# Two attention layers and two long convolutions: the second attention front in a fixed order, powers and reciprocals on ScalarE, the last norms row by row

## The chip, the cores and the metric

The kernel runs on one core of one Trainium2 chip. A core has a matrix engine (TensorE, PE in the profile, its weight loads PEld), three engines for elementwise work (VectorE or DVE, ScalarE or ACT, GpSimd or POOL) and SyncE (SP), whose queue issues nearly all DMA transfers here. Each engine takes its instructions in the order of its own queue and waits on semaphores for the others. The metric is the device time of one launch in microseconds (us), the median of several runs.

## The reference, cut to what matters

```python
def _A_ref(x, wqkv, wo):                      # S=2048, D=512, 32 heads of 16
    q, k, v = split(x @ wqkv)
    idx = pos[:, None] - 2 * arange(8)        # 8 keys, every second position back
    logits = einsum("bhsd,bhswd->bhsw", q, k[idx]) * 16 ** -0.5   # masked before 0
    attn = softmax(logits)
    return (einsum("bhsw,bhswd->bhsd", attn, v[idx])) @ wo

def _B_ref(u, A, B, C, log_dt, Dskip):        # L=2048, D=512, N=128
    K = einsum("dn,dnl,dn->dl", C, exp(dt * A * l), dt * B).real  # a kernel of length L
    return irfft(rfft(pad(u)) * rfft(pad(K)))[:L] + u * Dskip     # causal convolution

x = x + _A_ref(layernorm(x)); x = x + _B_ref(layernorm(x))
x = x + _A_ref(layernorm(x)); x = x + _B_ref(layernorm(x))
```

Both layers of a kind share their weights, so the convolution kernel and its spectrum are made once.

## The kernel before, in words

The residual x stays in SBUF as `x_sb`, 16 rows a = 0 to 15 of 128 positions by 512 features. Position is split as 16 p + a, so a shift by 2w positions is a shift by 2w rows of a tile, with 14 extra rows in front that hold the same data one partition further (`kT_ext`, `v_ext`).

**Attention, class `LayerA`.** The front works on blocks of four rows: statistics (`row_stats`), `ln_begin` (mean, variance, the power -0.5 by GpSimd, L103), `ln_end` (the shift `ln_nb`, L110), `ln_apply`, PE transposes (`front_t`), key projection with its evacuation to `kT` (`front_k`), and the shifted copy of the keys (`front_ext`). `core` then runs in two halves. The first takes quarters q of four rows and quarters ft of the features: DVE forms all products of queries and the 8 shifted keys (`mult`, tile `prod`), PE sums them per head into the logits L (`lsum`), and between them the projections of queries and values are dealt out by a fixed share (`proj`). For each quarter the maximum (`mx`), the exponential (`sub_exp`) and the normalisation (`norm_p`, with a DVE reciprocal, L334) follow. The second half loops over rows n = 0 to 15: DVE product `pv_mult(n)` (tile `pav`, two buffers), then on PE `pv_sum(n)` (tile `po`) and `out_proj(n-1)`, which adds the residual on PE. ScalarE takes the result back to `x_sb` with its sum and sum of squares; for rows 14 and 15 DVE takes the statistics (`bn_stats`, L77) and ScalarE copies. The next norm is woven in: `u_begin`, `u_end` and `u_apply` act on groups of rows 0-3, 4-7, 8-11, 12-13 and 14-15 and write `u`, the input of the convolution. In the first layer, a dictionary of events adds other work at named places of the loop: sine tables (`gx`, `gw`, `gs`), the load and reordering of the convolution kernel (`k_half_load`, `K`).

**Convolution, class `FftB`.** A Fourier transform as matrix products in two stages. `forward` walks steps s: `f1` (first stage, 16 matmuls into a PSUM tile of four buffers), evacuation by ScalarE or DVE (`evac`, by a running cost), `f2` 11 steps later, and for the data `u_f2` with two DVE products by the kernel's spectrum (`u_mult`, tiles t). In the first layer the kernel itself (`ka`) goes through the transform first, and each part of its spectrum is also written to DRAM. `kf_load` brings spectra to a ring of buffers, `ahead` of their use. `i1` and `i2` are the inverse stages; `i2` adds into `x_sb`. `middle` holds the inverse for the first half of the features.

**What sets the order.** Within `manual_schedule` the instructions of DVE, ScalarE, PE and SP run in the order in which the program emits them. That holds for all parts but one: the second attention front, between the first convolution and the second `core` (L1215 to L1229), is ordered by the framework. There each block of four rows is taken whole as its rows come out of `i2` (`rows_done`).

Of the kernel before, what the change touches and what calls it, by code (L numbers as in the profile page):

```python
# [19 lines left out]
P = 128  # L20
S = 2048
D = 512
# [5 lines left out]
EPS = 1e-5  # L28
MAN = {ET.DVE, ET.Activation, ET.PE, ET.SP}
# [12 lines left out]
EV = dict(act=0.93, dve=1.16)  # L42
# [32 lines left out]
def row_stats(nc, lnst, x_row, a, eng):  # L75
    if eng == "dve":
        nc.vector.bn_stats(lnst["bn"][:, a, :], x_row)  # L77
    else:
        nc.scalar.activation(lnst["junk"][:], x_row, ACT.Identity, accum_out=lnst["s1"][:, a:a + 1])
        row_sumsq(nc, lnst, x_row, a)  # L80
# [6 lines left out]
def ln_begin(nc, pool, lnst, a0, a1, eng):  # L87
    n = a1 - a0
    rstd = pool.tile([P, n], F32, name="ln_rstd")
    if eng == "dve":  # L90
        ag = pool.tile([P, n, 2], F32, name="ln_ag")
        for a in range(n):
            nc.vector.bn_aggr(ag[:, a, :], lnst["bn"][:, a0 + a, :])
        var, mean, ms = ag[:, :, 1], ag[:, :, 0], -1.0
    else:
# [5 lines left out]
        var = veps[:]  # L101
    nc.vector.tensor_scalar(rstd[:], var, EPS, None, ALU.add)  # L102
# [22 lines left out]
class LayerA:  # L125


    def __init__(self, tc, nc, consts, lnst, A_wqkv, A_wo, layer, xnT, nq):
# [10 lines left out]
        self.ps_l = self.wv = None  # L139

# [11 lines left out]
    def front_q(self, q):  # L152
        for ft in range(NDT):
            self.qproj1(q, ft, self.qT[q], self.ps_pj, "pp")

    def front_open(self):
# [5 lines left out]
        self.ps_pj = self.fctx.enter_context(tc.tile_pool(name=f"a{l}_ps_pj", bufs=2, space=PSUM, side="right"))  # L162
        self.nc.gpsimd.memset(self.kT[:, :, 0:14, 0:1], 0.0)
# [8 lines left out]
    def front_block(self, b, x_rows, st_eng, ln_eng, ev_eng, ext):  # L172
        nc, lnst = self.nc, self.lnst
        if st_eng == "dve":
            for a in range(4):
                row_stats(nc, lnst, x_rows[:, a, :], b * 4 + a, st_eng)
        self.front_apply(b, x_rows, ln_block(nc, self.fp, lnst, b * 4, b * 4 + 4, st_eng), ln_eng)
        self.front_t(b, ev_eng[0:2])
        self.front_k(b, ev_eng[2:])
        if ext is not None:  # L180
            for ft in range(NDT):
                self.front_ext(b, ext, ft)

    def front_apply(self, b, x_rows, rn, ln_eng, out=None):
        self.xn = self.fp.tile([P, 4, D], BF16, name="xn") if out is None else out
# [3 lines left out]
    def front_t(self, b, ev_eng):  # L189
        nc, xn = self.nc, self.xn  # L190
# [8 lines left out]
    def front_k(self, b, ev_eng, fts=range(NDT)):  # L199
        nc = self.nc  # L200
        for ft in fts:
            pp = self.ps_pj.tile([P, 512], F32, name="pp", tag="pp")
# [57 lines left out]
    def core(self, x_sb, u, ev=None, nprod=0):  # L260
# [14 lines left out]
        with ExitStack() as c2:  # L275
# [10 lines left out]
            ps_o = c2.enter_context(tc.tile_pool(name=f"a{l}_ps_o", bufs=2, space=PSUM))  # L286

# [36 lines left out]
            def norm_p(q):  # L324
# [6 lines left out]
                nc.vector.tensor_tensor(ssum[:], s2[:, :, 0:1, :], s2[:, :, 1:2, :], ALU.add)  # L331
                rs = wk.tile([P, 4, 1, H], BF16, name="rs")
                with nc.allow_low_precision("softmax normaliser in bf16 (attention weights are bf16)"):
                    nc.vector.reciprocal(rs[:], ssum[:])  # L334
# [25 lines left out]
            def out_proj(a):  # L360
# [6 lines left out]
                if a >= 14:  # L367
# [6 lines left out]
            def u_begin(a0, a1, eng):  # L374
                lns[a0] = (ln_begin(nc, wk, lnst, a0, a1, eng), a1)

            def u_end(a0):
                lns[a0] = (ln_end(nc, wk, lns[a0][0]), lns[a0][1])

            def u_apply(a0, rows):  # L380
                rstd, nb = lns[a0][0]
                for a in rows:
                    ln_apply(nc, u[:, :, a, :], x_sb[:, a, :].rearrange("p (q r) -> p q r", r=4), rstd, nb, a - a0,
                             "dve" if a % 2 else "act")
# [20 lines left out]
            for q, ft in slots:  # L405
                if q == 1 and ft == 0 and 1 not in self.qT:
                    while 1 not in self.qT or projs[0][0] is q_proj:
                        proj(1)
                mult(q, ft)
# [6 lines left out]
                if ft == 0 and q > 0:  # L416
                    proj(0.5)
                    acc -= 0.5
                    sub_exp(q - 1)
                if ft == 3 and q > 0:  # L420
                    norm_p(q - 1)
            proj(100)
            linit(3)
            for n in range(16):
# [3 lines left out]
                if n in (2, 10):  # L428
# [3 lines left out]
                if n in (6, 10):  # L432
                    u_begin(n - 6, n - 2, "act")
                if n in (7, 11):
                    u_end(n - 7)
                if n in (8, 9, 12, 13):
                    b0 = 0 if n < 10 else 4
                    r0 = b0 + (0 if n in (8, 12) else 2)
                    u_apply(b0, range(r0, r0 + 2))
                if n == 14:  # L440
                    u_begin(8, 12, "act")
# [11 lines left out]
            u_end(8)  # L453
            u_begin(12, 14, "act")
            out_proj(15)
            u_apply(8, range(8, 12))
            u_end(12)
            u_apply(12, range(12, 14))
            u_begin(14, 16, "dve")
            u_end(14)  # L460
            u_apply(14, range(14, 16))
# [143 lines left out]
class FftB:  # L605
# [72 lines left out]
    def kf_load(self, n):  # L678
# [10 lines left out]
        if self.kf_ring is None:  # L689
            self.kf_ring = [pool.tile([P, 4, 2, DQG, EC], BF16, name=f"kf_ring{i}")  # L690
                            for i, pool in enumerate((self.ring_pool, self.ring2))]
        kc = self.kf_ring[n // 4 % 2][:, n % 4]
# [64 lines left out]
    def forward(self, srcs):  # L757
# [3 lines left out]
        lag = NQT + 3  # L761
        self.kf = {}
        n_u = 0
        for s in range(len(F2) + lag):
            if s == lag + len(F2) - NG * NEC:
                for n in range(self.ahead):
                    self.kf_load(n)
            self.u_mult()
            if s < len(F1):
                self.f1(*F1[s])  # L770
            if s >= lag:
                key, g, ec = F2[s - lag]
                if key == "ka":
# [10 lines left out]
    def middle(self, done=None):  # L784
        self.i1(1, 0)
        self.i1(1, 1)
        for t in range(NA // 4):
# [4 lines left out]
            if done is not None:  # L792
                done(t)
# [321 lines left out]
def kernel(  # L1115
# [23 lines left out]
    with tc.tile_pool(name="ctmp", bufs=1) as tmp:  # L1139
        consts = build_a_consts(tc, nc, cpool, tmp)  # L1140
    lnst = dict(s1=cpool.tile([P, NA], F32, name="ln_s1"), s2=cpool.tile([P, NA], F32, name="ln_s2"),
                bn=cpool.tile([P, NA, 6], F32, name="ln_bn"), junk=cpool.tile([P, D], BF16, name="ln_junk"),
# [149 lines left out]
```

## Time and profile before

| | |
|---|---|
| median of 3 runs | 495.63 us (495.64, 492.5, 495.63) |
| profiled execution, its own time | 492.67 us |
| its span | 490.8 us |
| PE busy | 363.8 us (74%), granted clock 0.947 |
| DVE busy | 417.1 us (85%) |
| ACT busy | 332.6 us (68%) |
| POOL busy | 35.0 us (7%) |
| first kernel generation and first front | 0 to 128 us |
| first attention, its halves | 128 to 159, 159 to 228 |
| first convolution with the kernel's spectrum | 228 to 299 |
| second front | 299 to 332 |
| second attention, its halves | 332 to 369, 369 to 433 |
| second convolution | 433 to 491 |

The span is the time from the first to the last instruction; the launch adds 1.9 us to it here. Busy shares are means over stages with different limits, so the prediction reads each stage by itself. A line such as L354 is a line of the kernel printed above; "out<-in" names the tiles that an instruction writes and reads; the bracket behind a timeline row gives how long its engine was idle before it and what ended that.

### The profile page before, as it was taken

What the parts mean: (1) busy time and instruction counts of PE and PEld (TensorE: products, weight loads), DVE (VectorE), ACT (ScalarE), POOL (GpSimd) and SP (SyncE); (2) the same over time, 40 slices, a digit from 0 to 9 for tenths busy, and PEclk for the clock granted to TensorE, in tenths of its full rate; (3) what the DMA queues carried; (4) which work ended last, traced back from release to release, by engine and by line L of the source; (5) the groups of instructions that cost most, each with busy time, mean ns of one, the idle gap of its engine ahead of it and who ended that gap; (6) DMA issues with size and microseconds to landing.
All of it is one profiled execution on the core that took longest, in us unless ns stands there. A gap on an engine that the chain in (4) does not pass through costs nothing.

```text
span 490.8 us, 12670 instructions
## 1 busy us (share of the span) xinstructions
PE 363.8 (74%) x5434; PEld 273.6 (56%) x5470; DVE 417.1 (85%) x583; ACT 332.6 (68%) x535; POOL 35.0 (7%) x38
## 2 busy tenths in 40 slices
PE   1000237888999787796996894889997998958796
PEld 1000116564855666575985793444555686747795
DVE  7799979999999998985896968838999999748974
ACT  5999688856365667957897970674552557759873
POOL 2000102000000002121000000100000022210000
PEclk9999987999999899989899999799997899979899
DMA  8901610112015735522265523531022044022715
GB/s 219 369 1 21 65 43 1 45 19 54 9 22 158 243 96 186 229 61 87 94 236 182 188 84 98 162 116 56 3 77 74 2 174 172 1 87 77 233 61 152
DMA packets 57403, 52.22 MB, mean 106 GB/s; under 512 B 28829, under 2 KB 45826, under 8 KB 56066
## 3 DMA queue, kind: packets, MB, share of 16 engines
q1 hardware_dynamic: 57202, 51.27, 33.8%
q8 instruction: 43, 0.70, 0.6%
q10 hardware_dynamic: 144, 0.13, 0.2%
q14 instruction: 14, 0.11, 0.1%
HBM read 30.28 MB, written 13.24 MB: 89 GB/s over the span
## 4 chain that ended last, share of the span: by engine, by line
PE 44%; DVE 22%; ACT 18%; DMA 5%; issue 4%; SPq 3%; POOL 2%; DVEq 0%; ACTq 0%; POOLq 0%
PE pp L204 6%; PE po L354 6%; DVE pav L346 6%; PE pq L145 5%; PE pb L653 4%; PE pq L299 4%; DVE t L706 4%; PE pk L1039 3%; PE L L257 3%; PE pb L660 2%; DVE prod L250 2%; POOL ln_rstd L103 2%; PE pq L366 2%; ACT ws L957 2%; PE pb L732 2%
## 5 line engine op out<-in xcount | busy, mean ns | idle before, releaser
L354 PE MATMUL po<-ident,pav 128*128 128x128 bf16 x1024 | 67.1, 227 | 15.4 <-DVE pav L346 15.4
L354 PEld LDWEIGHTS <-pav 128*128 128x128 bf16 x1024 | 62.7, 102 | 23.6 <-DVE pav L346 20.2
L346 DVE TENSOR_TENSOR pav<-attn,v_ext 128x4096 bf16<-128x4096 bf16 x32 | 72.9, 2283 | 0.2 <-PE po L354 0.2
L250 DVE TENSOR_TENSOR prod<-qT,kT_ext 128x4096 bf16<-128x4096 bf16 x29 | 65.8, 2286 | 3.2 <-PE L L257 3.1
L103 POOL TENSOR_TENSOR ln_rstd<-ln_rstd,ln_mh 128x4 f32<-128x4 f32 (+1 forms) x18 | 29.4, 1632 | 280.4 <-DVE ln_rstd L102 234.5
L357 ACT CAST oT<-po 128x512 bf16<-128x512 f32 x32 | 18.5, 577 | 29.6 <-PE po L354 29.6
L204 PE MATMUL pp<-xnT,kT_ext 128*128 128x512 bf16 x124 | 32.6, 405 | 7.4 <-ACT xnT L197 5.9
L660 PE MATMUL pb<-a1s,w_sb 128*128 128x64 bf16 x768 | 31.3, 198 | 7.3 <-DVE a1s L642 4.4
L716 ACT CAST ub<-pb 128x1024 bf16<-128x1024 f32 x32 | 32.5, 1053 | 6.1 <-DVE t L706 5.9
L195 PE MATMUL pt<-ident,x_blk 128*128 128x128 bf16 x64 | 5.6, 241 | 41.5 <-ACT x_blk L120 41.5
L1039 PE MATMUL pk<-B_t,A_t 128*64 128x84 bf16 (+1 forms) x512 | 25.1, 209 | 12.5 <-issue 9.3
L731 PE MATMUL pb<-Wp,t 128*128 128x128 bf16 x256 | 31.9, 222 | 3.2 <-DVE t L706 2.3
L660 PEld LDWEIGHTS <-w_sb 128*128 128x128 bf16 x768 | 27.2, 101 | 10.5 <-DVE a1s L642 4.7
L301 ACT CAST v_ext<-pq 128x512 bf16<-128x512 f32 x32 | 18.7, 585 | 20.4 <-PE pq L299 20.4
L732 PE MATMUL pb<-WpJ,t 128*128 128x128 bf16 x256 | 31.6, 223 | 1.2 <-DVE t L706 1.1
L257 PEld LDWEIGHTS <-prod 128*128 128x128 bf16 x928 | 27.4, 96 | 8.9 <-DVE prod L250 2.7
L1039 PEld LDWEIGHTS <-A_t 128*64 128x64 bf16 (+1 forms) x512 | 22.9, 109 | 15.8 <-issue 12.6
L366 PE MATMUL pq<-wop,oT 128*128 128x512 bf16 x112 | 30.4, 386 | 1.0 <-issue 0.2
L145 PE MATMUL pq<-xnT,kT_ext 128*128 128x512 bf16 x120 | 29.6, 381 | 0.6 <-issue 0.3
L642 DVE CAST a1s<-pb 128x1024 bf16<-128x1024 f32 x21 | 25.0, 1222 | 5.8 <-PE pb L653 5.7
L299 PE MATMUL pq<-wv,xnT 128*128 128x512 bf16 x120 | 29.6, 379 | 0.4
L642 ACT CAST a1s<-pb 128x1024 bf16<-128x1024 f32 x27 | 26.8, 1024 | 4.2 <-PE pb L653 3.5
(211 smaller groups left out, 862.6 us busy)
## 6 DMA issues: line engine op xcount, KB each, us to landing
w_sb<-w_dram SPq DMA_DIRECT2D x8, 1024.0 KB
w_dram<-w_zero SPq DMA_DIRECT2D x1, 4096.0 KB
kf_ring<-kf_dram SPq DMA_DIRECT2D x16, 256.0 KB
kf_ring<-kf_dram SPq DMA_DIRECT2D x32, 128.0 KB
v_ext<-v_ext SPq DMA_DIRECT2D x4, 784.0 KB
x_blk<-in_A_x_dram SPq DMA_DIRECT2D x4, 512.0 KB
kT_ext<-in_A_wqkv_dram SPq DMA_DIRECT2D x4, 512.0 KB
x_sb<-in_A_x_dram SPq DMA_DIRECT2D x4, 512.0 KB
```

The lines of the kernel that those rows point to most:

```text
L145: nc.tensor.matmul(pq[:], lhsT=self.wqk[:, dt, ft * P:(ft + 1) * P], rhs=self.xnT[:, dt, q * 512:(q + 1) * 512], start=(dt == 0), stop=(dt ...
L204: nc.tensor.matmul(pp[:], lhsT=self.wqk[:, dt, D + ft * P: D + (ft + 1) * P], rhs=self.xnT[:, dt, b * 512:(b + 1) * 512], start=(dt == 0), ...
L250: nc.vector.tensor_tensor(pr, self.qT[q][:, ft].unsqueeze(1).to_broadcast([P, W, 4, P]), kap, ALU.mult)
L257: self.nc.tensor.matmul(L[:, al, w, ft * 8:(ft + 1) * 8], lhsT=pr[:, w, al, :], rhs=self.c["ind8"][:], start=False, stop=True, skip_group_ ...
L299: nc.tensor.matmul(pp[:], lhsT=xnT[:, dt, a * P:(a + 1) * P], rhs=wv[:, dt, :], start=(dt == 0), stop=(dt == NDT - 1))
L346: nc.vector.tensor_tensor(pv[:], attn[:, n % 4].unsqueeze(2).to_broadcast([P, W, DH, H]), vap, ALU.mult)
L354: nc.tensor.matmul(po[:, ft, :], lhsT=pvf[:, w, ft * P:(ft + 1) * P], rhs=ident[:], start=(w == 0 and ft == 0), stop=(w == W - 1), skip_gr ...
L366: nc.tensor.matmul(pw[:], lhsT=oT[:, ftp, :], rhs=wo[:, ftp, :], start=False, stop=(ftp == NDT - 1))
L642: (nc.scalar.copy if eng == "act" else nc.vector.tensor_copy)(dst, src)
L660: nc.tensor.matmul(p2[:, j, :], lhsT=self.w2[:, ec * EC + j, :], rhs=a1s[:, ec * EC + j, :], start=True, stop=True)
L732: nc.tensor.matmul(p3[:, j, :], lhsT=t2[:, dql, :], rhs=wpj_r, start=False, stop=True)
L1039: nc.tensor.matmul(o, lhsT=lhs, rhs=Bt[:, ri, c * CH + ql].rearrange("p b g -> p (b g)"), start=(not half and j % 4 == 0 and ri == 0), sto ...
```

## The change

- **Powers on ScalarE.** `ln_begin` can take the power as Ln (with the epsilon as bias) and Exp (scale -0.5) on ScalarE; in the loops all groups but rows 0-3 do, and the whole second front. The softmax reciprocal becomes Ln and Exp (scale -1). It moves with the three adds ahead of it into `recip`, one or two products earlier than the rest of `norm_p`. The table set that holds both functions is loaded by an instruction written out at two places.
- **Last norms.** Groups become 0-3, 4-7, 8-10, 11-12 and then single rows 13, 14, 15. `u_begin` and `u_end` stand together where ScalarE has the power. Row 13's statistics are taken by DVE too. In the first layer the single rows are handed to `forward` and run behind its steps 1 to 3.
- **Second front.** Written out by hand: statistics in halves (`half_stats`), the first half inside `middle`; two of the four `i2` of the second half add on PE and evacuate on ScalarE; blocks are interleaved; one of two transposed tiles per block is evacuated by DVE; the last block's keys and the first queries go into the first four slots of `core`.
- **Spectra.** `kf_load` starts four steps earlier in the first layer with `ahead` 4; the ring of the second layer has 7 slots instead of 8. Some events of the first loop are one place earlier, the first sine behind the kernel load.

```diff
-EV = dict(act=0.93, dve=1.16)
+EV = dict(act=0.93, dve=1.2)
...
+def half_stats(nc, lnst, x_sb, t, g):
+    for a in range(4 * t, 4 * t + 4):
+        nc.vector.bn_stats(lnst["bn"][:, a, g, :], x_sb[:, a, g * (D // 2):(g + 1) * (D // 2)])
...
+    if rs == "act":
+        nc.scalar.activation(rstd[:], var, ACT.Ln, bias=EPS)
+        nc.scalar.activation(rstd[:], rstd[:], ACT.Exp, scale=-0.5)
+        return rstd, mean, ms
...
-            def norm_p(q):
+            def recip(q):
...
+                ls = wk.tile([P, 4, H], F32, name="ls")
+                nc.scalar.activation(ls[:], ssum[:, :, 0, :], ACT.Ln)
                 rs = wk.tile([P, 4, 1, H], BF16, name="rs")
-                with nc.allow_low_precision("softmax normaliser in bf16 (attention weights are bf16)"):
-                    nc.vector.reciprocal(rs[:], ssum[:])
+                nc.scalar.activation(rs[:, :, 0, :], ls[:], ACT.Exp, scale=-1.0)
+                st[q]["rs"] = rs
+
+            def norm_p(q):
+                ex, rs = st[q]["ex"], st[q]["rs"]
                 attn = wk.tile([P, 4, W, H], BF16, name="attn", bufs=3)
...
-                if a >= 14:
+                if a >= 13:
                     row_stats(nc, lnst, pw[:], a, "dve")
...
+                event(("m", q, ft))
                 mult(q, ft)
...
+                if ft == 1 and q > 0:
+                    recip(q - 1)
                 if ft == 3 and q > 0:
                     norm_p(q - 1)
...
-                if n in (2, 10):
+                if n in (1, 9):
+                    recip(2 + n // 8)
+                if n in (3, 11):
                     norm_p(2 + n // 8)
...
-                if n in (6, 10):
-                    u_begin(n - 6, n - 2, "act")
-                if n in (7, 11):
-                    u_end(n - 7)
-                if n in (8, 9, 12, 13):
+                if n == 6:
+                    u_begin(0, 4, "act")
+                if n == 10:
+                    u_begin(4, 8, "act", "act")
+                if n in (7, 10):
+                    u_end(0 if n == 7 else 4)
+                if n in (8, 9, 11, 12):
...
+                if n == 13:
+                    u_begin(8, 11, "act", "act")
+                    u_end(8)
                 if n == 14:
-                    u_begin(8, 12, "act")
+                    u_apply(8, range(8, 11))
+                if n == 15:
+                    u_begin(11, 13, "act", "act")
+                    u_end(11)
+                    u_apply(11, range(11, 13), "dve")
...
+            def finish(a0, a1):
+                u_begin(a0, a1, "dve", "act")
+                u_end(a0)
+                u_apply(a0, range(a0, a1), "dve")
+
+            if l == 0:
+                out_proj(15)
+                return [lambda a=a: finish(a, a + 1) for a in (13, 14, 15)]
+            finish(13, 14)
             out_proj(15)
...
+            finish(14, 15)
+            finish(15, 16)
...
-            self.kf_ring = [pool.tile([P, 4, 2, DQG, EC], BF16, name=f"kf_ring{i}")
+            self.kf_ring = [pool.tile([P, 4 - i, 2, DQG, EC], BF16, name=f"kf_ring{i}")
                             for i, pool in enumerate((self.ring_pool, self.ring2))]
-        kc = self.kf_ring[n // 4 % 2][:, n % 4]
+        kc = self.kf_ring[n % 7 // 4][:, n % 7 % 4]
...
+            if s > 0 and late:
+                late.pop(0)()
             if s >= lag:
                 key, g, ec = F2[s - lag]
+                if s == max(lag, lag + len(F2) - NG * NEC - 4):
+                    for n in range(self.ahead):
+                        self.kf_load(n)
...
+        ev = {("v", 1): [x_load], ("o", 1): [lambda: k_half_load(0), G(gw, 0), G(gs, 0), G(gx, 1)],
+              ("m", 1, 0): [lambda: nc.scalar.preload_act_table_set(EXP_LN)],
+              ("p", 0): [G(gx, 0)],
...
-    fb.ahead = 3
+    fb.ahead = 4
...
+        fb.middle(lambda t: half_stats(nc, lnst, x_sb, t, 0))
+        fb.swap_psum()
+        la.front_open()
...
+        def stats(b):
+            half_stats(nc, lnst, x_sb, b, 1)
+            ln[b] = ln_begin(nc, lnp, lnst, 4 * b, 4 * b + 4, "dve", "act", 2)
+
+        def norm(b):
+            la.front_apply(b, x_sb[:, b * 4:(b + 1) * 4, :], ln_end(nc, lnp, ln[b]), ["dve"] * 4)
...
+        fb.i2(1, 0)
+        fb.i2(1, 1, "act")
+        stats(0)
+        fb.i2(1, 2, "act")
+        norm(0)
+        stats(1)
+        fb.i2(1, 3)
+        la.front_t(0, ("act", "dve"))
+        norm(1)
+        stats(2)
+        keys(0, (0, 1))
+        la.front_t(1, ("act", "dve"))
+        keys(0, (2, 3))
+        norm(2)
+        stats(3)
+        la.front_ext(0, "dve")
+        keys(1, (0, 1))
...
+        def last(ft):
+            keys(3, (ft,))
+            la.qproj1(0, ft, la.qT[0], la.ps_pj, la.pj_tag)
+            la.front_ext(3, "dve", ft)
+
+        ev = {("m", 0, ft): [lambda ft=ft: last(ft)] for ft in range(NDT)}
```

## The prediction

> **What bounds the kernel now.** Read first, the busy time in windows: one row a stage, start:end, then busy us of PE, PEld, DVE, ACT and POOL, granted clock, DMA share, GB/s.
>
> ```profile
> 159.00:228.00 69.00, 56.62 (x729) 43.36 (x735) 60.95 (x66) 49.37 (x100) 9.65 (x7) 0.95 0.48 159
> 299.00:332.00 33.00, 24.75 (x146) 12.74 (x148) 22.41 (x71) 17.02 (x25) 4.03 (x4) 0.90 0.50 143
> 365.00:433.00 68.00, 60.64 (x803) 45.94 (x809) 61.13 (x61) 37.39 (x86) 9.31 (x4) 0.92 0.24 86
> ```
>
> These are the token loop (rows n = 0 to 15) of the first attention, the second front, and the second loop. In the loops DVE and PE are both about 0.9 busy: each waits for the other in places, so it is the order that decides. The front fills no engine. Next, waits (us in all, times, longest), of DVE and PE in 145 to 232 and of PE in 285 to 345:
>
> ```profile
> DVE ln_nb L110 <- POOL ln_rstd L103: 2.7, 3, 0.9
> PE po L354 <- DVE pav L346: 9.7, 9, 2.4
> PE pt L195 <- DVE xn L122: 4.5, 1, 4.5
> ```
>
> Last, the timeline (start, us; idle time before in brackets), PE rows 11 and 15, DVE's two ends of the second loop, and two marks of the fronts:
>
> ```profile
> 209.48 3.37 PE L354 MATMUL po<-ident,pav 128*128 128x128 bf16 x32 [2.39 <-DVE pav L346]
> 427.90 1.95 PE L354 MATMUL po<-ident,pav 128*128 128x128 bf16 x32
> 416.95 2.28 DVE L346 TENSOR_TENSOR pav<-attn,v_ext 128x4096 bf16<-128x4096 bf16 x1
> 424.73 2.28 DVE L346 TENSOR_TENSOR pav<-attn,v_ext 128x4096 bf16<-128x4096 bf16 x1
> 430.96 0.70 DVE L77 BATCH_NORM_STATS2 ln_bn<-pq 128x6 f32<-128x512 f32 x1 [3.95 <-PE pq L366]
> 305.19 2.21 PE L195 MATMUL pt<-ident,xn 128*128 128x128 bf16 x16 [4.53 <-DVE xn L122]
> 332.51 2.29 DVE L250 TENSOR_TENSOR prod<-qT,kT_ext 128x4096 bf16<-128x4096 bf16 x1
> ```
>
> A row's steps, start to start in these views: product pav 2.20 on DVE, sum po 1.79 and projection 1.08 on PE, copy 0.5 and two statistics passes 1.35 on ACT. After pav 15 DVE has nothing that PE waits for: PE runs on unbroken from row 11 to the end at 431.84. The row-11 line shows what a gap of 2.4 costs besides: po takes 3.37 instead of 1.95, with 0.60 of the clock granted in 209 to 213.
>
> **1. Reciprocal and powers to ScalarE.** Eight DVE reciprocals (0.95, 0.99 to the next start) become Ln and Exp on 128x128; the nearest ACT row of that size takes 0.31. The three adds move up one or two products, so DVE no longer waits in line for the result, but they now wait for ex: by the old times ex of the first two groups ends 0.7 and 1.8 us after the products ahead of the adds (350.92 against 350.2; 152.5 against 150.7), so those two reciprocals per layer give nearly nothing: the first pav starts 0.4 earlier in layer 0, 1.0 in layer 1. Norm powers: POOL's 1.0 to 3.2 us become Ln and Exp on 128x4, 0.19 to 0.23 each by ACT's smallest rows. But ACT is a queue: in front of the Ln at row 10 stand the projection evacuations of row 8, so DVE's ln_nb waits some 0.8 there, as it waited 0.9 for POOL.
> Table loads: the before shows 1.28 each; two are written out now where two were inserted, so none is added. If Ln and Exp did not share a table, 24 pairs would load up to 48 times.
>
> The Trainium skill ("ScalarE: Activation LUTs", What ACT_TABLE_LOAD costs) charges each switch a load of 1.28 and a drain of 1.38. The row agrees on the load; the Exp behind it starts 0.02 later, so no drain shows; by the page a thrash would cost twice as much.
>
> **2. Layer 0's loop.** Up to the end of pav 12 DVE loses two reciprocals (2.0), the 0.96 wait for g_i at 185.51 (its sine is set behind the 18 k loads, but SP is free from 161.8, so they issue early), 0.4 at the start, 0.3 of small terms: 3.65, so pav 12 ends at 208.95 instead of 212.6. Should the loads start as late as before, a DMA of 3.64 stands in front of ACT instead.
>
> Then the two waits that the change adds. **Row 13:** the norm of rows 8 to 10 is begun and ended at once. Its Ln is queued on ACT behind both passes of row 11, these behind po 12 and projection 11. DVE waits in ln_nb, and pav 14 behind it. **Row 14:** row 13's statistics are now taken by DVE (a >= 13), so bn_stats 13 stands on DVE ahead of pav 15 and waits for projection 13, which waits for po 14. PE has only po 15 next, and waits for bn_stats and pav 15. The chain from the end of pav 12, all from rows above: po 12 and projection 11 2.87, ACT 1.35, Ln and Exp 0.45, ln_nb 0.2, k copy 0.33, pav 14 2.2, po 14 and projection 13 2.87, bn_stats 0.76, pav 15 2.2, po 15 1.79, two projections 2.16: **17.2**, against 226.5 - 212.6 = 13.9. PE is idle about 3 us ahead of po 15, longer than the 2.39 that slowed row 11; I add 1.6 for a slow po (3.37 - 1.79). Layer 0: -3.65 + 3.3 + 1.6 = **+1.2** (-1.5 with DVE further ahead and no slowing, +3).
>
> "TensorE: Matmul & The Clock Gate" of the Trainium skill (Part 1: The HAM clock gate) has the clock fall after an idle window of about 3.4 us. Here 2.39 was enough; by the page the 1.6 might fall away.
>
> **3. Last norms behind the transform.** Before, PE starts the transform at 228.22, fills four buffers and idles to 232.62, for the norms hold up both evacuating engines until 231.2 and 231.6; then eight tiles at half clock take it to 238.03. After, evacuations start at once, but each of three rows is a round trip (aggregate 0.1, Ln, Exp 0.4, ln_nb 0.15, apply 0.37, handoffs 0.2: 1.2) in which DVE and ACT wait on each other in turn, with the next evacuations queued behind. I get the twelfth tile at 238 again: **0** (-2.3, the old gap less overlap, to +1.5).
>
> **4. Kernel-spectrum loads.** In layer 0 they start four steps sooner. Before, DVE waited 2.6 and 1.5 for them. But SP issues at 0.64 a load and is already filled by the spectrum writes (0.97 of every 1.14): the fifth load then sets the pace. **-1.3** (-4.1 to 0). In layer 1 the ring shrinks from 8 slots to 7, so the eighth load waits for the first product; SP issues a set in 1.92 us against products of 1.2, and the sets from the 13th on land about 1 late: **+1.0** (0 to +1.9).
>
> **5. The second front.** Half the statistics move into the middle stage, into DVE's 1.2 to 1.4 waits for PE: 4 of 0.34 each time, hidden; without that cover 5.4. From the first add of the second half (297.3) DVE then does, in order: two adds 2.3, 16 half statistics 5.4, aggregates 1.8, norms 5.8, four copies from PSUM at 1.14 (nearest: the f32 PSUM cast; the lower bound is 0.6, a 512 PSUM row), shifts 1.65: 21.6, and 3.3 of waits for Ln/Exp and key evacuations: 322.2. The mask matmuls follow (1.0). Then per product: key 0.86, query 0.86, query evacuation 0.6, product 2.3, sums 0.8: 5.47, with PE idle 1.2 of it, since the product waits for the query and the sums for the product. Four: 345.1, against 346.7 before. The first product comes 7 us sooner (325.6), and most of it is given back in those four slots: **-1.6** (-8 if nothing is given back, +1.5 with the copies late and the clock low).
>
> **6. Layer 1's loop.** The same chain without the k copy: 16.9, against 431.84 - 419.15 = 12.7, so +4.2, and 1.6 for the clock. Ahead of pav 12 DVE gains the last reciprocal and a part of the 1.0 at the start, the rest lies under PE, which is continuous from 382 to 414: -1.5. Then one row at a time to the transform, 6.1 against 6.3 from projection 14: -0.2. **+4.1** (0 to +6).
>
> The cost figure for evacuation (1.16 to 1.2) moves about one cast a stage from DVE (1.14) to ACT (0.91), under PE's pace of 0.57 a tile, and the second statistics tile and the pools issue nothing: 0.
>
> **Sum:** 1.2 + 0 - 1.3 + 1.0 - 1.6 + 4.1 = +3.4. The profiled execution took 492.67 (span 490.8 and 1.9 around it), so 496.1; it lies 3.0 under the median, at the low one of the two levels that the runs show (492.5 and 495.6). Half way between the levels: **497.6**.
>
> **Rivals.** *The order pays* (faster): DVE gets 3.9 of reciprocals back per layer, the PSUM copies cost 0.6, the loads their full 4.1, the clock stays up in both ends: -1.6 - 1.6 (clock) - 2.8 (loads) - 2.2 (copies) from the sum, and 2 less in row 13: about 487. For it: DVE's 61 of 69 in the loop. Against: the wait at row 14 is there whatever DVE saves. *The clock* (slower): each new PE gap, ahead of po 14 and po 15 in both loops and in the four slots, sets the clock to half as at row 11: two gaps of 1.6 more in the loops and 4 in the slots: +7, 505. It decides where a gap over 2 falls; against it, the 1.90 gap at 416.03 left po at 1.96. *Tables thrash*: 61 us of ACT, perhaps 25 on the path, 523; against it the one set written out by name.
>
> **How the numbers follow.** Forecast 0.55, order 0.2, clock 0.2, thrash 0.05. A measurement of this kernel tells about 1% (5 us) from no change. Of the forecast's 0.55, by its own spread (-2 to +8 around the sum's +3.4), 0.40 lies within 1%, 0.14 above and 0.01 below; with the rivals, same 0.40, slower 0.39, faster 0.21. The range goes from the order's time to the clock's, one level either way: 486 to 507.
>
> **What would show it.** Right: a PE gap of about 3 ahead of po 15 in both loops, with bn_stats as what DVE waited for; DVE waits of 1.5 to 2 in ln_nb at row 13; four lsum gaps of about 1.2 behind a first product near 325; five table loads; the transform no faster to its twelfth tile. Wrong: a loop end under 226 or 431 after like starts, no gap ahead of po 15, or the front's sums done before 342.

## The result: 3 to 4% slower, and the profile after

The changed kernel takes **510.94 us** (508.18 to 512.84, 4 runs) against 495.57 for the kernel before: ratio **1.032** (95% interval 1.025 to 1.039). Measured again beside the last experiments it took 511.46 against 493.26: 1.037 (1.031 to 1.042). Three of the kernels below had one or two runs in a slower state of the chip; their medians and all ratios leave these runs out. The forecast was 497.6 with a range up to 507: wrong. The profiled execution took 512.36 with a span of 510.4, 19.6 more than the span before. Mark by mark, from the timelines of both (us):

| stretch | before | after | difference | predicted |
|---|---|---|---|---|
| start to the end of projection 15, first loop | 226.70 | 239.02 | **+12.3** | +1.2 |
| to the first spectrum product (last norms) | 31.23 | 32.28 | +1.1 | 0 |
| to the first add of the middle stage (loads) | 29.16 | 27.66 | -1.5 | -1.3 |
| to product 0 of the second loop (middle, front, first half) | 82.88 | 83.71 | +0.8 | -1.6 |
| second loop, to the first transform matmul | 67.06 | 71.31 | +4.3 | +4.1 |
| to the first spectrum product, layer 1 | 10.38 | 10.24 | -0.1 | (in it) |
| to the end (ring) | 43.39 | 46.18 | +2.8 | +1.0 |

Five of six terms lie within 2.4 of the forecast; the first loop alone misses by 11. The windows of the two loops after (same columns as before):

```profile
158.45:240.42 81.97, 61.68 (x759) 47.22 (x764) 60.40 (x64) 53.34 (x110) 5.37 (x4) 0.90 0.42 135
378.00:450.00 72.00, 61.38 (x809) 45.70 (x814) 59.87 (x57) 40.58 (x98) 2.91 (x1) 0.95 0.24 86
```

DVE does no more than before (60.4 in the first, 61.0 before); on DVE the added time is idle time. PE is idle for 7.9 more and busy for 5.1 more, 61.68 instead of 56.62, with 0.90 of the clock granted instead of 0.95. The waits in 145 to 242 say where (us in all, times, longest):

```profile
DVE ln_bn L78 <- PE pq L374: 8.2, 3, 4.9
DVE ln_nb L121 <- ACT ln_rstd L111: 7.0, 3, 5.9
DVE g_i L621 <- ACT g_i L618: 3.6, 2, 2.3
PE po L362 <- DVE pav L354: 12.5, 10, 3.7
```

In 378 to 452 the same two DVE waits are smaller:

```profile
DVE ln_bn L78 <- PE pq L374: 5.7, 2, 2.9
DVE ln_nb L121 <- ACT ln_rstd L111: 4.3, 4, 2.1
```

The timeline, put in order of time, reads as one story: ScalarE's copy waits for a load, the statistics and the power stand behind the copy, DVE's `ln_nb` waits for the power, the product behind it is late, and the statistics of row 13 then wait for the sum of that product.

```profile
218.54 1.04 ACT L1212 COPY k_perm<-k_rl 128x1024 bf16<-128x1024 bf16 x1 [3.57 <-DMA k_rl<-kd_dram]
221.78 0.16 DVE L121 SCALAR_TENSOR_TENSOR ln_nb<-ln_s,ln_rstd 128x3 f32<-128x3 f32 x1 [5.91 <-ACT ln_rstd L111]
224.83 3.59 PE L362 MATMUL po<-ident,pav 128*128 128x128 bf16 x32 [3.67 <-DVE pav L354]
230.33 0.70 DVE L78 BATCH_NORM_STATS2 ln_bn<-pq 128x6 f32<-128x512 f32 x1 [4.89 <-PE pq L374]
233.27 3.58 PE L362 MATMUL po<-ident,pav 128*128 128x128 bf16 x32 [2.98 <-DVE pav L354]
```

The two lines with [5.91] and [4.89] are the two places that the prediction named; the first is three times its size, since the load was not in the sum. The chain that ended last carries the load too, and the sine's write (start, us, what):

```profile
175.70 4.29 DMA g_dram<-g_s
...
214.42 4.05 DMA k_rl<-kd_dram
222.57 2.21 DVE pav L354
224.83 3.59 PE po L362 x32
```

### The profile page after: what moved, and what is told of

Same layout as the page of the kernel before. It is cut to its first block, busy times and chain, and to the rows that moved or that the text cites. A ratio compares the mean times of both kernels' runs of the same rounds, so it can differ in the third digit from the quotient of the medians.

```text
span 510.4 us, 12694 instructions
## 1 busy us (share of the span) xinstructions
PE 372.1 (73%) x5442; PEld 278.1 (54%) x5478; DVE 413.0 (81%) x584; ACT 336.2 (66%) x571; POOL 18.7 (4%) x26
## 4 chain that ended last, share of the span: by engine, by line
PE 37%; ACT 23%; DVE 22%; DMA 8%; issue 4%; SPq 4%; DVEq 0%; ACTq 0%
PE po L362 6%; PE pp L205 5%; DVE pav L354 5%; DVE prod L251 4%; PE pq L302 3%; PE pk L1067 3%; PE pb L679 3%; PE pq L157 3%; PE L L258 3%; PE pq L374 3%; DVE t L732 3%; DMA kf_ring<-kf_dram 2%; ACT a1s L668 2%; ACT ln_junk L85 2%; ACT ws L985 2%
## 5 line engine op out<-in xcount | busy, mean ns | idle before, releaser
L362 PE MATMUL po<-ident,pav 128*128 128x128 bf16 x1024 | 70.3, 233 | 20.9 <-DVE pav L354 20.7
L362 PEld LDWEIGHTS <-pav 128*128 128x128 bf16 x1024 | 65.3, 105 | 30.8 <-DVE pav L354 29.2
L757 PE MATMUL pb<-Wp,t 128*128 128x128 bf16 x256 | 34.5, 232 | 5.4 <-DVE t L732 4.0
L758 PE MATMUL pb<-WpJ,t 128*128 128x128 bf16 x256 | 34.1, 232 | 1.8 <-DVE t L732 1.8
L742 ACT CAST ub<-pb 128x1024 bf16<-128x1024 f32 x32 | 32.4, 1066 | 3.4 <-DVE t L732 2.9
L157 PE MATMUL pq<-xnT,kT_ext 128*128 128x512 bf16 x122 | 31.2, 393 | 0.7 <-issue 0.5
L258 PE MATMUL L<-ind,prod 128*128 128x8 bf16 x928 | 27.6, 166 | 5.4 <-DVE prod L251 5.4
L668 ACT CAST a1s<-pb 128x1024 bf16<-128x1024 f32 x28 | 28.1, 1031 | 4.7 <-PE pb L679 4.4
L208 ACT CAST kT_ext<-pp 128x512 bf16<-128x512 f32 x32 | 18.6, 587 | 17.0 <-PE pp L205 16.7
```

The source lines that it names most:

```text
L157: nc.tensor.matmul(pq[:], lhsT=self.wqk[:, dt, ft * P:(ft + 1) * P], rhs=self.xnT[:, dt, q * 512:(q + 1) * 512], start=(dt == 0), stop=(dt ...
L258: self.nc.tensor.matmul(L[:, al, w, ft * 8:(ft + 1) * 8], lhsT=pr[:, w, al, :], rhs=self.c["ind8"][:], start=False, stop=True, skip_group_ ...
L362: nc.tensor.matmul(po[:, ft, :], lhsT=pvf[:, w, ft * P:(ft + 1) * P], rhs=ident[:], start=(w == 0 and ft == 0), stop=(w == W - 1), skip_gr ...
L668: (nc.scalar.copy if eng == "act" else nc.vector.tensor_copy)(dst, src)
L757: nc.tensor.matmul(p3[:, j, :], lhsT=t1[:, dql, :], rhs=wp_r, start=True, stop=False)
```

## The experiments

Theory: the loop ends are lost to waits in the queues of ScalarE and DVE that stand ahead of a product; what stands there is work that could run later. Rivals: the sine and the loads on SP's queue; the granted clock; the front. "First loop" and "second loop" below are from the start of product 0 to the end of projection 15, from each run's profile; ratios are to the kernel before on the same chip.

| kernel | median us | ratio (95%) | first loop | second loop |
|---|---|---|---|---|
| before | 493.3 to 495.6 | 1 | 67.7 | 62.0 |
| changed; again | 510.94; 511.46 | 1.032; 1.037 | 80.6; 80.4 | 66.7; 65.2 |
| 1 first sine ahead | 513.42 | 1.040 (1.036 to 1.045) | 80.9 | 66.5 |
| 2 copies one row later | 507.76 | 1.027 (1.023 to 1.031) | 73.8 | 66.7 |
| 3 row 13 on ScalarE | 505.11 | 1.021 (1.017 to 1.025) | 77.2 | 62.0 |
| 4 norm ended a row later | 503.74 | 1.022 (1.018 to 1.025) | 74.2 | 65.1 |
| 5 all four moves | 496.70 | 1.006 (1.003 to 1.009) | 70.0 | 60.3 |
| 6 two sine buffers | 512.22 | 1.037 (1.034 to 1.041) | 80.5 | 66.7 |
| 7 PE kept busy | 510.17 | 1.033 (1.030 to 1.036) | 79.1 | 66.5 |
| 8 before, ring of 7 | 496.29 | 1.004 (1.001 to 1.006) | 67.8 | 62.0 |
| 9 rows and sine (2+3+4+6) | 496.16 | 1.005 (1.003 to 1.008) | 68.4 | 60.3 |
| 10 as 9, norms in the core | 494.48 | 1.000 (0.997 to 1.002) | 69.0 | 61.7 |
| 11 as 9, old front | 493.49 | 0.999 (0.997 to 1.002) | 67.7 | 60.3 |
| 12 as 9, reciprocal on DVE, old places | 501.97 | 1.016 (1.012 to 1.020) | 69.3 | 63.5 |
| 13 candidate | **490.25** | **0.990 (0.987 to 0.994)** | 69.2 | 61.7 |

The loop columns are of one profile each. Two profiles of the changed kernel differ by 1.5 in the second loop, so smaller differences of two profiles say little by themselves.

**1. The first sine ahead of the loads.**

```diff
-("o", 1): [lambda: k_half_load(0), G(gw, 0), G(gs, 0), G(gx, 1)],
+("o", 1): [lambda: k_half_load(0)],  ("p", 1): [G(gw, 0), G(gs, 0), G(gx, 1)],
```

> The changed kernel with the first sine table again in its old place, ahead of the 18 loads of the convolution kernel on SP's queue. Theory (SP's order): in the profile after, ScalarE waits 3.1 in rows 4 to 6 for the transfer of the first sine, DVE 2.3 and 1.3 behind it, and PE's sum and projection there run slow; these waits should be gone or under 1, product 12 of the first loop should end near 209.5 instead of 212.7, and the total fall by about 3 (about 508). The wait for the second half of the convolution kernel at row 13 should stay near 3.6, since its loads follow a copy that moves with the rows. Rival (the clock): rows 4 to 6 are slow for the granted clock, and the wait only fills time that is lost anyway: product 12 ends where it did, total within 1 of the changed kernel (about 511).

The theory of the order fell: no gain. SP's queue in the changed kernel, and then in this run with ScalarE's wait (SP rows: start, time in which the issues were made, number):

```profile
162.40 13.19 SPq L1137 DMA_DIRECT2D k_rl<-kd_dram  x17
175.70 14.82 SPq L626 DMA_DIRECT2D g_dram<-g_s  x4
```

```profile
170.46 0.61 SPq L626 DMA_DIRECT2D g_dram<-g_s  x1
171.12 0.61 SPq L1121 DMA_DIRECT2D k_rl<-kd_dram  x1
171.77 9.95 SPq L1137 DMA_DIRECT2D k_rl<-kd_dram  x17
181.82 10.32 SPq L626 DMA_DIRECT2D g_dram<-g_s  x3
185.87 1.06 ACT L625 ACTIVATE g_s<-g_i 128x1024 bf16<-128x1024 int32 x1 [5.70 <-DMA g_dram<-g_s]
```

One write gets ahead, the loads start 9 later, and the second write stands behind them: ScalarE waits 5.70 instead of 3.13. With one sine buffer, either order puts a write behind the 18 issues of the loads.

**2. The copies of the second half one row later.**

```diff
-("p", 12): [lambda: k_half_fix(1), K(1, 0)], ("p", 13): [K(1, 1), K(1, 2)], ("p", 14): [K(1, 3)]
+("p", 13): [lambda: k_half_fix(1), K(1, 0)], ("p", 14): [K(1, 1), K(1, 2)], ("p", 15): [K(1, 3)]
```

> The changed kernel with the four copies of the second half of the convolution kernel, and the fix ahead of them, each one row later (rows 13, 14, 15 instead of 12, 13, 14). Theory (the copy blocks ScalarE): the copy no longer waits for its load in front of row 11's statistics, so DVE's wait in ln_nb at row 13 falls from 5.9 to about 2.2, PE's gap ahead of sum 14 from 3.7 to about 1, sum 14 takes about 2 instead of 3.6; the first loop ends 4 to 5 sooner, total about 506. Rival (the row-14 wait decides): PE loses nothing net, as the statistics of row 13 on DVE wait for the same projections anyway, and the end moves by under 1.5.

As expected in place: the longest `ln_nb` wait is 2.1, and PE's gap ahead of sum 14 shrinks:

```profile
221.93 1.96 PE L362 MATMUL po<-ident,pav 128*128 128x128 bf16 x32 [1.59 <-DVE pav L354]
```

The first loop is 6.8 shorter, more than expected. The total falls by less, by 3.2 from the first measurement of the changed kernel and by 5.1 in ratio from the second; in this profile the first loop begins 1.5 later, and the stretch between the loops takes 1.3 more.

**3. Row 13's statistics on ScalarE.** `a >= 14` in `out_proj`, and its `finish` fed from the sums.

> The changed kernel with row 13's statistics again on ScalarE, in both layers (a >= 14 instead of a >= 13), its norm fed from these sums. Theory (a wait in a queue ahead of the product): DVE no longer waits for projection 13 before product 15 (4.9 in the first layer), PE's gap of 2.98 ahead of sum 15 goes to under 0.5 in both layers, sum 15 takes about 2 instead of 3.6; 3 to 5 a layer, total about 503. Rival (the ends are bound by PE's clock or by ScalarE): the statistics passes add 0.8 to ScalarE ahead of row 14's evacuation and the loops end within 1.5 of the changed kernel, total 509 or more.

Confirmed in place: the loops are 3.4 and 4.7 shorter, and the second is as long as before the change; the total, 505.1, is 2 above what was expected. Waits of DVE in 145 to 242:

```profile
DVE ln_nb L121 <- ACT ln_rstd L111: 10.3, 4, 5.8
...
DVE ln_bn L78 <- PE pq L374: 0.4, 1, 0.4
```

The statistics wait is gone (8.2 before the edit); part of it comes back as a longer wait in `ln_nb` behind the last product, which holds nobody. The wait of 5.8 at row 13 is untouched.

**4. The norm of rows 8 to 10 ended a row later.** The changed kernel itself ran beside it.

```diff
                 if n == 13:
                     u_begin(8, 11, "act", "act")
-                    u_end(8)
                 if n == 14:
+                    u_end(8)
                     u_apply(8, range(8, 11))
```

> The changed kernel with the norm of rows 8 to 10 ended one row later, behind product 14, and nothing else. Theory (a round trip through ScalarE ahead of a product): product 14 no longer stands behind ln_nb, so it starts 2.1 sooner in the second loop and about 6 sooner in the first, where sum 14 then waits for the copies on ScalarE instead (3.6 sooner); total 4 to 6 under the changed kernel (505 to 507). Rival (only the three edits together pay, as the statistics of row 13 hold product 15 anyway): under 2 below the changed kernel.

> The changed kernel itself, unchanged, as the base of the single edits on this chip: both theories expect 510 to 512, a ratio of 1.032 to 1.037.

7.7 under the changed kernel beside it by the medians, 7.5 by the ratios: over the upper end of what was expected. In the first loop DVE now meets the late load itself, but product 14 waits 2.6 for it instead of 5.9:

```profile
218.75 0.43 DVE L1212 COPY k_perm<-k_rl 128x1024 bf16<-128x1024 bf16 x1 [2.64 <-DMA k_rl<-kd_dram]
219.09 2.29 DVE L354 TENSOR_TENSOR pav<-attn,v_ext 128x4096 bf16<-128x4096 bf16 x1
222.03 0.16 DVE L121 SCALAR_TENSOR_TENSOR ln_nb<-ln_s,ln_rstd 128x3 f32<-128x3 f32 x1 [0.65 <-ACT ln_rstd L111]
```

The gain lies in the first loop, 6.4. In the second, the gap ahead of sum 14 goes (1.40 in the changed kernel), but sum 15 stays behind its gap of 2.98 and takes 3.44: the loop is 65.1, as in the second profile of the changed kernel (65.2).

**5. All four moves.**

> The three edits together (first sine ahead, copies one row later, row 13's statistics on ScalarE), and as a fourth the norm of rows 8 to 10 ended one row later, behind product 14. Theory: no engine waits at rows 13 and 14 of either loop; PE runs without a gap over 1.5 from row 11 to the loop's end, as in the kernel before; first loop 10 to 13 shorter, second 5 to 6, total about 493 to 496. Rival (the clock or the front): the waits come back in the last norms and at the transform's start, or the front and the middle keep part of the loss: total 500 or more.

The rows account for nearly the whole loss: 1.032 to 1.037 falls to 1.006, and the total is 0.7 above the upper end of what was expected. The second loop is now 1.8 shorter than before the change, the first still 2.3 longer. Alone, edits 2, 3 and 4 took 6.8, 3.4 and 6.4 off the first loop and the sine's move added 0.4; together they took off 10.6: the waits overlap.

**6. Two sine buffers.** `bufs=2` on the tile that the sines are written to.

> The changed kernel with the sine table in two buffers, so that the second sine doesn't wait for the transfer of the first; nothing else. Putting the sine back in its old place took nothing off, as there the later writes stood behind the 18 loads on SP's queue and ScalarE waited 5.7 at row 5. Theory (SP's queue and one buffer): either order makes ScalarE wait; with two buffers the 3.1 on ScalarE and the 2.3 and 1.3 of DVE in rows 4 to 6 fall to under 1 in all, product 7 of the first loop starts near 189.5 instead of 192.5, and about 3 is taken off the total (508). Rival (the wait moves on): the third sine waits for the same queue, or the copies of the convolution kernel at row 6 wait for loads: product 7 moves by under 1.

The wait went, the time stayed. ScalarE waits for no DMA in rows 2 to 6; product 7 comes 32.4 after product 0 instead of 34.1. But product 12 starts 51.9 after product 0, against 52.1, and the loop is as long as it was. In this profile the sums of rows 7 and 10 take 3.33 and 2.94, and the rows behind give the gain back. So the wait in rows 4 to 6 was real, and taking it away by itself gained nothing.

**7. PE kept busy ahead of sum 15.** The 12 extra matmuls stand behind projection 13.

> The changed kernel with 12 extra matmuls of 128x512 (2.6 us, result unused) on PE behind projection 13 in both loops, in the gap of 2.98 ahead of sum 15. The waits of the engines stay as they are. Theory (the clock follows the gap): sum 15 takes 1.96 instead of 3.58 and 2.43, projection 14 too is fast; the first loop ends 1.6 to 2.3 sooner, the second 0.5 to 1; total about 508. Rival (the clock falls for another reason, or the fill is itself in the way): sum 15 as slow as before, or it starts later by what the fill overruns; total 511 or more.

```profile
230.94 2.91 PE L477 MATMUL pq<-x_sb,ident 128*128 128x512 bf16 x11
234.13 1.96 PE L362 MATMUL po<-ident,pav 128*128 128x128 bf16 x32 [0.28 <-DVE pav L354]
```

The sum takes 1.96 instead of 3.58 with the same wait of DVE: the slowness follows PE's idle time. The sum itself is 1.6 shorter, the first loop 1.5, the second 0.3 shorter or 1.3 longer than in the two profiles of the changed kernel; in the total it can't be told from that kernel's two results. At this place the clock follows the wait, and it is worth 1.6 of the 12.3; no run keeps PE busy ahead of sum 14.

**8. The kernel before with 7 ring slots.** The ring's second tile has 3 slots, and the slot is `n % 7`.

> The kernel before with 7 slots instead of 8 in the spectrum ring of the second convolution, and nothing else. Prediction's step: the loads from the thirteenth on land about 1 late, +1.0 in all. Theory from the last profiles: a wait of 0.7 to 1.7 in the last products makes a gap on PE ahead of the last inverse-stage matmuls, which then run at 0.31 instead of 0.22 us for some 3 us; so +2 to +3. Rival: the loads are hidden, under 0.5.

0.4% slower, 1.9 (0.6 to 3.1). DVE's wait, then the windows behind it, first of this run and then of the kernel before:

```profile
DVE t L706 <- DMA kf_ring<-kf_dram: 1.4, 4, 0.4
```

```profile
470.00:474.00 4.00, 2.51 (x26) 2.38 (x27) 2.38 (x4) 1.31 (x2) 0.00 (x0) 0.76 0.00 1
474.00:478.00 4.00, 4.00 (x52) 3.69 (x50) 1.72 (x3) 1.95 (x2) 0.00 (x0) 0.81 0.02 4
```

```profile
470.00:474.00 4.00, 3.45 (x52) 3.07 (x49) 2.35 (x4) 2.81 (x3) 0.00 (x0) 1.00 0.00 0
474.00:478.00 4.00, 4.00 (x68) 3.91 (x65) 3.33 (x3) 1.71 (x2) 0.00 (x0) 1.00 0.26 70
```

The loads are 1.4 late in all, within what was priced (1.0, up to 1.9). PE then waits 1.45 for the last product and works at a granted clock of about 0.8 instead of 1.00; the stretch to the end grows by 2.9 in this profile, twice the wait.

**9. Rows and sine.**

> The changed kernel with the copies one row later, row 13's statistics on ScalarE, the norm of rows 8 to 10 ended one row later (these three as in the run of four moves), the first sine left behind the loads, but in two sine buffers. Theory: rows 4 to 6 lose their waits too (4.4 on DVE in the run of four moves), so the first loop ends 3 to 5 sooner than there: total 491 to 493, under the kernel before by 0.3 to 0.8%. Rival (another engine holds rows 4 to 8): the loop ends within 1 of the run of four moves, total 496.

A miss in the total: the first loop is 1.7 shorter than in run 5, the total hardly (496.2 for 496.7). The total is the rival's. No transfer holds ScalarE in rows 2 to 6 now, but it works without a pause from 173.0 to 192.2, and DVE waits there for `g_i`, the sines' arguments that ScalarE makes, 3.1 in two places instead of 4.4 in one:

```profile
178.29 0.69 DVE L621 TENSOR_SCALAR g_i<-g_i 128x1024 int32<-128x1024 int32 x1 [2.30 <-ACT g_i L618]
```

What remains against the kernel before is mostly outside the loops, which the next runs take apart.

**10. The last norms in the core again.** As in the second layer, `finish` runs for all three rows ahead of the transform.

> The kernel of the last run (three row edits and two sine buffers), with the norms of rows 13 to 15 of the first layer again ahead of the transform, as in the second layer. In the five runs with late norms the time from the first transform matmul to the first spectrum product is 30.9 to 31.8, in the kernel before 29.7. Prediction's step: 0 (-2.3 to +1.5). Theory (late norms hold both evacuating engines): the transform begins later, but the first spectrum product comes 1 to 2 sooner; total 494 to 495.5, against 496.2. Rival (the late norms are hidden): first spectrum product at the same time, 0.

Confirmed: 1.7 less by the medians, 2.8 by the ratios (1.1 to 4.4). In the profiles the transform starts 2.1 later (231.42 for 229.34) and its first spectrum product comes 1.9 sooner (259.25 for 261.17).

**11. The front of the kernel before.**

> The kernel of the last run (three row edits and two sine buffers), with the second front and the middle stage of the kernel before: blocks taken whole, statistics not in halves, first queries and last keys inside the front. From the first add of the middle to the first row of the second loop the kernels with the new front take 83.7 to 84.5, the kernel before 82.9. Theory (the front's gain is given back in the four slots and in the middle, and more than that): the total falls by about 1, to 495.2. Rival (the prediction's -1.6): it rises by 1.6, to 497.8.

2.7 less by the medians, 2.9 by the ratios (1.3 to 4.5): more than expected. From the first add of the middle to product 0 of the second loop it is 82.3 instead of 83.9; where the rest lies was not found.

**12. The reciprocal on DVE again.**

> The kernel of the last run (three row edits and two sine buffers), with the softmax reciprocal on DVE again (0.95 each, eight of them) at its old places. Theory (DVE sets the rows of both loops once the new waits are gone): loops get back what they gained, 1.5 to 2 in each layer; total 498 to 500 against 496.2. Rival (the reciprocal lies beside PE's work): within 1 of 496.2.

5.8 more by the medians, 5.1 by the ratios (2.9 to 7.4): the part of the change that pays. By the profiles 0.9 lies in the first loop, 1.3 in the stretch from the middle to the second loop and 3.3 in the second loop. The run puts back the places too, of the adds and of `norm_p` (rows 2 and 10 instead of 3 and 11), so it doesn't tell the engine from the order.

**13. Candidate.** The changed kernel with the edits of run 9, and with the front, the ring of 8 and the place of the last norms as before. From its edit (the copies of run 2 are in it too):

```diff
-                if a >= 13:
+                if a >= 14:
...
                     u_begin(8, 11, "act", "act")
+                if n == 14:
                     u_end(8)
-                if n == 14:
                     u_apply(8, range(8, 11))
...
-        gs = tmp.tile([P, 2, 4, P], BF16, name="g2_s")
+        gs = tmp.tile([P, 2, 4, P], BF16, name="g2_s", bufs=2)
```

> Candidate: of the change it keeps the reciprocals and powers on ScalarE, the row groups of the loops with the three row edits, two sine buffers, and the earlier spectrum loads with four ahead; the second front, the norms ahead of the transform and the ring of 8 slots are as in the kernel before. Sum of the parts from the runs: 496.2 less 1.6 (late norms), 1.0 (front) and 1.9 (ring) = 491.7, or 0.995 of the kernel before. Rival (the parts don't add, as each time another engine ends last): 494 or more, no faster than before.

490.25, **1.0% faster than the kernel before** (0.6 to 1.4%) and some 4% faster than the changed one; 491.7 was expected from the single runs, so within the noise the parts add. Against the kernel before its profile has the second loop at 61.7 instead of 62.0, the stretch from first spectrum product to middle 2.7 shorter, the first loop still 1.5 longer (again with slow sums at rows 7 and 10, 3.37 and 2.98; run 11, with the same three row edits, took 67.7). So against the kernel before it is the earlier spectrum loads that show as a gain, and no run has them alone; in the loops the reciprocals' saving only makes good another loss: in run 12, which lacks the saving, the loops are 1.6 and 1.5 longer than in the kernel before. What costs this much was not taken apart.

## Why the prediction was right or wrong

- **Layer 0's loop, +1.2: the step that failed, by 11.** It has two mis-sized terms.
  - *Up to pav 12, -3.65:* product 12 started at 210.53 against 210.40, nothing gained. Two of its parts were read wrongly. "SP is free from 161.8, so they issue early" was right about the start (161.67) and took the loads as done when they started; they kept SP for 13.9 and the sine's write stood behind them. The wait of 3.64, which the text kept for loads that start late, came all the same, as 3.13. And the reciprocals, counted as 2.0: up to row 12 the first loop gains nothing from their move (product 12 starts 51.1 after product 0 with them on DVE in run 12, 51.5 with them on ScalarE in run 9). In run 9 DVE waits 3.1 for ScalarE's `g_i` there, in run 12 0.8. The wait of 2.2 for `ex` in the profile after lies ahead of product 0, where the prediction had put it.
  - *From pav 12, +3.3 and 1.6:* from the start of product 12 to the end of the loop it was 28.5, against 16.3 before: 12.2 more, not 4.9. The chain was the right one, but "k copy 0.33" was one of DVE's; the copy on ScalarE, with a load not yet landed, was not followed. It makes 3.8 of the miss (5.91 in `ln_nb`, 2.08 in run 2, where the copy comes later). The clock came in twice, at sums 14 and 15, not once: sum 14 and the projection behind it took 2.4 longer than at full speed, with 0.53 of the clock granted from 224.0 to 230.3.
  - Runs 2, 3 and 4 confirm each of the three waits by taking it away.
- **Layer 1's loop, +4.1: right, in both parts** (2.9 in the second profile). Product 12 came 1.7 sooner behind product 0 (1.5 foretold), and what follows it took 6.4 longer (5.8 foretold; 4.7 in the second profile). The wait in `ln_nb` was 2.07, the gap ahead of sum 15 2.98, and run 3 brings the loop back to the 62.04 of before.
- **Late norms, 0: mis-sized.** Run 10 puts them at +1.7 to +2.8, the profiles of the result at +1.1, about the upper end of -2.3 to +1.5 or above it. In the profile after, DVE waits 0.50 to 0.54 in each of the three norms and ScalarE up to 1.90 for the aggregate, with evacuations queued behind.
- **Loads, -1.3: right** (-1.5 in the profile; no run has them alone). **Ring, +1.0: the wait right, its follower left out**: +1.9.
- **Front, -1.6: wrong in sign.** The first product came at 338.54, 28.1 after the add at 310.46, against 35.3 before: 7.2 sooner, as foretold. The four slots give 7.0 of it back: from the first product to the last sums of the fourth slot it was 21.3, where the prediction's sum has 19.5 and the kernel before 14.3. And the half statistics in the middle were not hidden: its adds took 1.4 longer. Between two adds DVE now casts `z` as well (1.21, at 304.20), and that left no wait for the statistics (1.41 behind each add); in run 11, with such a cast but without half statistics, the adds took only 0.3 longer. Run 11 puts front and middle together at +2.7 to +2.9. Two of the four gaps of 1.2 on PE came, the others were 0.5 and 0.4:

```profile
340.89 0.95 PE L258 MATMUL L<-ind,prod 128*128 128x8 bf16 x32 [1.33 <-DVE prod L251]
345.15 2.29 DVE L251 TENSOR_TENSOR prod<-qT,kT_ext 128x4096 bf16<-128x4096 bf16 x1 [1.41 <-ACT qT L159]
353.20 0.95 PE L258 MATMUL L<-ind,prod 128*128 128x8 bf16 x32 [1.28 <-DVE prod L251]
```

- **The reciprocal** was credited with some 4 over both layers; run 12 shows 5.1 to 5.8, with its places.
- **The start, 497.6 rather than 496.1:** the two levels of the kernel before do not show in more runs. On the chips of the experiments it took 490.0 to 497.9, most runs between 492 and 496 and in no two groups.
- **The rivals.** *The order pays* did not come, for the named reason (the wait at row 14 is there whatever DVE saves). *The clock* was right that a new gap can slow PE, but run 7 shows it as worth 1.6 at one place; that its total of 505 lies nearer to the result than the forecast is chance. *Thrash* did not come: five table loads, as foretold and as before.

## What to carry to other kernels

A step moved behind another on one engine must be followed through every queue that both use: here a load issued early kept the issuing queue busy, and a copy for a later stage sat in ScalarE's queue ahead of a power that a product waited for. Put a norm's round trip through a second engine behind the next product, not ahead of it, and take statistics on the engine that writes the row, not on the one that sets the pace. A front that delivers its first result sooner was worth nothing here, as the work cut off it was dealt out in slots where each product waited for it.

## What the runs showed of the hardware that was not expected

- **The same idle time on PE doesn't always slow the work behind it.** Ahead of sum 15 in the second loop, the gap of 2.98 gave sums of 2.43 and, in the second profile of the same kernel, 1.96; in the first loop 3.58. A gap of 2.38 left a sum at 1.96 in run 3, 2.39 gave 3.37 before. A gap of 1.45 was followed by a granted clock of 0.76 to 0.81 in run 8. Neither the 2.39 of the prediction nor the idle window of 3.4 that the Trainium skill gives in "TensorE: Matmul & The Clock Gate" (Part 1: The HAM clock gate) separates these cases; what else decides stays open.
- **DVE copies bf16 from PSUM in 0.69** for 128x1024 (0.60 from start to start; table of the front's groups after), against 1.22 for the f32 cast of that size: the lower bound of the prediction, not the 1.14 that it took. "VectorE: DVE Perf Modes" in the Trainium skill (Why PSUM operands drop a tier) caps a PSUM operand at its 2x mode, and at 1x for fp32; the two times, 0.69 and 1.22, agree with that order.

```profile
L198 DVE COPY xnT<-pt 128x1024 bf16<-128x1024 bf16 x4 | 2.8, 688 | 3.3 <-PE pt L196 3.3
```
